# Residual rows by a DRAM copy, a bias row by accumulating DMAs, and a margin behind the products in TensorE's order

## The chip, the cores and the metric

The kernel runs on one core of one Trainium2 chip. The time is the device time of one execution in microseconds (us). Profiles are of one execution each; their times count from the start of the profiled span.

## The reference

One layer in which attention and a dense branch run side by side on the same normalised input (S = 2048 tokens, D = 640, bf16):

```python
xn = layernorm(x)                        # over D
# A: 32 heads of width 20; each position looks at 8 positions, 2 apart, backwards
q, k, v = split(xn @ wqkv)
logits[h,s,w] = (q[h,s] . k[h,s-2w]) * 20**-0.5      # s-2w < 0 is masked
o[h,s] = sum_w softmax_w(logits)[h,s,w] * v[h,s-2w]
# B: dense, F = 1536
h = gelu(xn @ w1 + b1)
out = x + o @ wo + h @ w2 + b2
```

The change concerns the terms `x + ... + b2` and the place of the logits in TensorE's queue.

## The kernel before

The 2048 tokens are cut into four chunks (`NCH`, number n) of 512, and each chunk into four blocks (`BPC`, number bl) of 128 tokens. The last of the 16 blocks has the number `LASTB` = 15. Everything between the first loads and the last store is held as small pieces of work, each with a name, an engine, an estimated duration, a rank, the pieces it needs and the buffers it holds. `make_plan` lists them; `Plan.run` plays them through with these numbers, at each moment giving a free engine the ready piece of lowest rank, and so fixes the order of TensorE, VectorE and ScalarE. That order is issued as it is (`manual_schedule` with these three engines). When a piece really takes longer than its estimate, the queues don't rearrange: the engine stands at the piece whose turn it is. SP (plain DMAs) and GpSimd, called POOL in profiles, are not in that set. Of a piece's needs on another engine the plan adds a small lag (0.22, 0.08 and 0.1 us behind TensorE, VectorE and ScalarE).

The pieces of a chunk, with their names:

- `st`, `rs`, `rc`, `xn`: mean and variance, square root, reciprocal, normalised rows (VectorE, ScalarE). `tp`, `tc`: transposes on TensorE and their copy to SBUF (`xnT`).
- `pj`, `pc` (chunk 0: `gj`, `gc`): the projections q, k, v (L428 and L445 in the profile) and their eviction. `pad`: the 14 columns ahead of a chunk's k and v, copied from the chunk before, or set to zero by a memset on POOL (L468) for chunk 0.
- `qk`: for each of the 8 offsets a product of q with the shifted k on VectorE (L478, tile `prod`). `lg`: four pieces per chunk, each sums two such products per head on TensorE into the logits `L` (L490).
- `m`, `mx`, `ex`, `ss`, `ri`, `at`: the softmax (maximum on VectorE L513, exponential on ScalarE, sum on TensorE L538, reciprocal and product on VectorE).
- `xd`: four DMAs from SP that spread the weights over the partitions of the heads' columns (L559, tile `ax`; there is one buffer of it).
- `av`, `ad`, `ot`: weights times shifted v (L569), additions (L578), and the attention output `oT` (L584), on VectorE.
- `f1`, `ge`: the dense branch's first product (L591) and GELU (L602). `o`: five pieces per block that accumulate h @ w2 and o @ wo in PSUM (L623, L624). `oc`, `od`: eviction to `osb` and the store.

The terms x and b2 come in at two places. Piece `xb` (one per chunk, L403) adds the broadcast row b2 to the chunk's x in SBUF, and for blocks below `LASTB` SP then stores the result to the output (L412, 15 stores in all). `od` later adds each block's `osb` to these rows by an accumulating DMA from POOL (L636). For the last block, x + b2 goes into PSUM by a product with the identity instead, and `osb` is stored plainly. So each piece `o` of a chunk needs `xb` of that chunk.

The loads stand at the start, ahead of the identity matrix and the constants that POOL makes (L317 to L325 and the helper make_identity). SP issues, in this order: x of chunk 0 and wqkv, b1, the rest of x, w1, the row b2 to all partitions (`b2bc`), w2, wo.

Of the kernel before, what the change touches and what calls it, by code (L numbers as in the profile page):

```python
# [11 lines left out]
ALU = mybir.AluOpType  # L12
# [3 lines left out]
PE, VE, SE, DQ = "pe", "ve", "se", "dq"  # L16


class Plan:
# [13 lines left out]
    def pool(self, name, n):  # L33
        self.pools[name] = n

    def add(self, name, engine, us, rank, needs, fn, bufs=(), after=0.0, table=None):
        t = {
            "name": name,
            "eng": engine,
            "us": us,  # L40
            "rank": rank,
            "needs": list(needs),
            "fn": fn,
            "bufs": list(bufs),
            "after": after,
            "table": table,
            "i": len(self.tasks),
        }
        self.tasks.append(t)
        self.by[name] = t  # L50
        for b in bufs:
            self.bufs.setdefault(b, set()).add(name)
        return name

    def run(self):
        end, left, held = {}, list(self.tasks), {p: {} for p in self.pools}
        remaining = {b: set(u) for b, u in self.bufs.items()}
        free = {PE: 0.0, VE: 0.0, SE: 0.0, DQ: 0.0}
        now, started, table = 0.0, [], "sqrt"
        running = []  # L60
        while left:
            done = [t for t in running if t["end"] <= now + 1e-9]
            for t in done:
                running.remove(t)
                for b in t["bufs"]:
                    remaining[b].discard(t["name"])
                    if not remaining[b]:
                        held[b[0]].pop(b, None)
            moved = True
            while moved:  # L70
                moved = False
                for eng in (PE, VE, SE, DQ):
                    if free[eng] > now + 1e-9:
                        continue
                    best = None
                    for t in left:
                        if t["eng"] != eng or t["after"] > now:
                            continue
                        if best is not None and (t["rank"], t["i"]) >= (best["rank"], best["i"]):
                            continue  # L80
                        if any(
                            n not in end
                            or end[n] + (self.LAG[self.by[n]["eng"]] if self.by[n]["eng"] != eng else 0.0) > now + 1e-9
                            for n in t["needs"]
                        ):
                            continue
                        new = {}
                        for b in t["bufs"]:
                            if b not in held[b[0]]:
                                new[b[0]] = new.get(b[0], 0) + 1  # L90
                        if any(len(held[p]) + k > self.pools[p] for p, k in new.items()):
                            continue
                        best = t
                    if best is not None:
                        left.remove(best)
                        best["start"], best["end"] = now, now + best["us"]
                        if best["table"] not in (None, table):
                            table = best["table"]
                            best["end"] += self.TABLE
                        end[best["name"]] = best["end"]  # L100
                        free[eng] = best["end"]
                        for b in best["bufs"]:
                            held[b[0]][b] = True
                        running.append(best)
                        started.append(best)
                        moved = True
            nxt = [f for f in free.values() if f > now + 1e-9]
            nxt += [
                e + self.LAG[self.by[n]["eng"]]
                for n, e in end.items()  # L110
                if e + self.LAG[self.by[n]["eng"]] > now + 1e-9
            ]
            nxt += [t["after"] for t in left if t["after"] > now + 1e-9]
            if left and not nxt:
                raise RuntimeError("no piece can start: " + ", ".join(t["name"] for t in left[:8]))
            if left:
                now = min(nxt)
        return started


S, D, F, H, W, DIL = 2048, 640, 1536, 32, 8, 2
P = 128
DH = D // H
PAD = (W - 1) * DIL
KT, FT = D // P, F // P
CH = 512
NCH = S // CH
BPC = CH // P
# [5 lines left out]
LASTB = S // P - 1  # L134
# [5 lines left out]
def make_plan(fns):  # L140

    pl = Plan()
# [6 lines left out]
    def f(kind, *a):  # L149
        return lambda: fns[kind](*a)  # L150
# [6 lines left out]
    for n in range(NCH):  # L157
        base = n * PERIOD
# [4 lines left out]

        for bl in range(BPC):
            land = (3.2, 3.2, 6.6, 6.6)[bl] if n == 0 else 11.4 + 1.9 * n
            pl.add(f"st{n}{bl}", VE, 1.1, -40 if n else -99, [], f("st", n, bl), after=land)
            if n == 0:
                pl.add(f"rs{n}{bl}", SE, 0.35, -99, [f"st{n}{bl}"], f("sqrt", n, bl, bl + 1), table="sqrt")
                pl.add(f"rc{n}{bl}", VE, 0.17, -99, [f"rs{n}{bl}"], f("rstd", n, bl, bl + 1))
# [3 lines left out]
        for bl in range(BPC):  # L173
            xn, tp = ("xn", n, bl), ("acc", "tp", n, bl)
            pl.add(f"xn{n}{bl}", VE, 0.42, early - 4 if n else -99, [f"rc{n}{bl}" if n == 0 else f"rc{n}"], f("xn", n, bl), [xn])
            pl.add(f"tp{n}{bl}", PE, 0.3, early - 3 if n else -99, [f"xn{n}{bl}"], f("tp", n, bl), [xn, tp])
            pl.add(f"tc{n}{bl}", SE, 0.65, early - 3 if n else -99, [f"tp{n}{bl}"], f("tc", n, bl), [tp, xnT])
        pl.add(f"xb{n}", VE, 1.5, base + 30, [f"xn{n}{bl}" for bl in range(BPC)], f("xb", n), after=31.0)

        if n == 0:  # L180
            for bl in range(BPC):
                for g, parts in enumerate(GROUPS):
                    ps, last = ("acc", "g", bl, g), max(p[0] for p in parts)
                    tos = sum(p[2] - p[1] for p in parts)
                    land = (5.9, 9.2, 11.5)[last]
                    r = -50 + (last == 2)
                    pl.add(f"gj{bl}{g}", PE, 0.28 * tos, r, [f"tc0{bl}"], f("gj", bl, g), [xnT, ps], land)
                    pl.add(f"gc{bl}{g}", SE, (0.27, 0.54, 0, 0.54)[tos - 1], -50, [f"gj{bl}{g}"], f("gc", bl, g), [ps] + [(q, k, v)[p[0]] for p in parts])
        for which, buf in enumerate((q, k, v)):
            for to in range(KT if n else 0):  # L190
                ps = ("acc", "p", n, which, to)
                r = early + (0 if which < 2 else 20)
                pl.add(f"pj{n}{which}{to}", PE, 1.08, r, [f"tc{n}{bl}" for bl in range(BPC)], f("pj", n, which, to), [xnT, ps])
                pl.add(f"pc{n}{which}{to}", SE, 0.52, early, [f"pj{n}{which}{to}"], f("pc", n, which, to), [ps, buf])
            if which:
                need = done(n - 1, which) if n else []
                bufs = [buf] + ([("k" if which == 1 else "v", n - 1)] if n else [])
                pl.add(f"pad{n}{which}", SE, 0.26, early if n else -50, need, f("pad", n, which), bufs)

        L = ("L", n)  # L200
        for wp in range(W // 2):
            pr = ("prod", "qk", n, wp)
            for i in range(2):
                need = done(n, 0) + done(n, 1) + [f"pad{n}1"]
                pl.add(f"qk{n}{wp}{i}", VE, 1.47, base + 3 * wp + i, need, f("qk", n, wp, i), [q, k, pr])
            pl.add(f"lg{n}{wp}", PE, 0.6, n - 1000, [f"qk{n}{wp}{i}" for i in range(2)] + ([f"lg{n}{wp-1}"] if wp else []), f("lg", n, wp), [pr, L])

        e, at, ax = ("e", n), ("attn", n), ("ax", n)
        m, rs, ss = ("m", n), ("rs", n), ("acc", "ss", n)
# [9 lines left out]
        for wp in range(W // 2):  # L219
            for i in range(2):  # L220
                need = [f"xd{n}", f"pad{n}2"] + done(n, 2)
# [11 lines left out]
        for bl in range(BPC):  # L233
            ob = ("osb", n, bl)
            O = [("O", n, bl)] if n < NCH - 1 or bl % 2 == 0 else [("acc", "lo", n, bl), ("acc", "hi", n, bl)]
            last = None
            for pc in range(5):
                need = [last] if last else [f"ge{n}{ft}" for ft in range(FT)] + [f"xb{n}"]
                if pc == 4:
                    need.append(f"ot{n}")  # L240
                us = (0.82, 0.82, 0.82, 1.1 if (n, bl) == (NCH - 1, BPC - 1) else 0.82, 1.37)[pc]
                last = pl.add(f"o{n}{bl}{pc}", PE, us, base + PERIOD + 8 + 8 * bl, need, f("o", n, bl, pc), O + (hTs if pc == 0 else hTs[3 * pc : 3 * pc + 3] if pc < 4 else [oT]), 31.0)
            pl.add(f"oc{n}{bl}", SE, 0.78, base, [last], f("oc", n, bl), O + [ob])
            pl.add(f"od{n}{bl}", SE, 0.0, base, [f"oc{n}{bl}"], f("od", n, bl), [ob])
# [4 lines left out]
def kernel(  # L249
# [16 lines left out]
    nc = tc.nc  # L266
    assert tuple(A_x.shape) == (1, S, D) and tuple(B_w1.shape) == (D, F)

    x_sd = A_x.rearrange("b s d -> (b s) d")
# [36 lines left out]
        cs = slice(n * BPC, (n + 1) * BPC)  # L306
        nc.sync.dma_start(x_sb[:, cs, :], x_nb[:, cs, :])
    nc.sync.dma_start(w1_sb[:], B_w1.rearrange("(t p) n -> p t n", p=P))
    nc.sync.dma_start(b2bc[:], b2_bcast)
    nc.sync.dma_start(w2_sb[:], B_w2.rearrange("(t p) n -> p t n", p=P))  # L310
    nc.sync.dma_start(wo2[:], A_wo.rearrange("(p t) n -> p t n", t=KT))


    ident = consts.tile([P, P], BF16, name="ident")
# [83 lines left out]
            tiles["tp", n, bl][:, 0 : KT * P].rearrange("p (t m) -> p t m", t=KT),  # L398
        )

    def do_xb(n):
        cs = slice(n * BPC, (n + 1) * BPC)
        nc.vector.tensor_tensor(  # L403
            out=x_sb[:, cs, :],
            in0=x_sb[:, cs, :],
            in1=b2bc[:].unsqueeze(1).to_broadcast([P, BPC, D]),
            op=ALU.add,
        )
        for bl in range(BPC):
            b = n * BPC + bl  # L410
            if b < LASTB:
                nc.sync.dma_start(out_sd[b * P : (b + 1) * P, :], x_sb[:, b, :])  # L412


    def qkv_tile(n, which):
# [259 lines left out]
```

## Time and profile before

| | us |
|---|---|
| median of three runs | 235.9 |
| lowest and highest of them | 233.46 and 236.65 |
| the profiled execution | 233.1 |
| its span | 231.1 |

| engine | busy us | share of the span |
|---|---|---|
| TensorE, products | 213.3 | 92% |
| VectorE | 171.7 | 74% |
| ScalarE | 109.2 | 47% |
| GpSimd | 14.5 | 6% |

PE is TensorE, PEld its weight load, DVE VectorE, ACT ScalarE; "SPq" is SP's queue. A line such as "PE L L490 <- DVE prod L478: 4.6, 3, 2.6" in the list of waits says that TensorE stood for 4.6 us in three places before instructions of line 490 until VectorE had finished those of line 478, at most 2.6 us at once. In the chain of waits (the work that ended last, followed back from the end) each line has a start, a duration and what took the time. In the timeline the number in brackets is the time for which the engine was idle just before, and who ended that. Of the rows of slices, each digit is a fortieth of the span (5.8 us) in tenths of busy time.

### The profile page before, as it was taken

The numbers are of one execution on the slowest core, as the hardware profiler recorded it, in microseconds if no ns is written. First come the engines' busy times: TensorE is split into PE (matmuls) and PEld (weight loads), VectorE is DVE, ScalarE is ACT, GpSimd is POOL, SyncE is SP. The second block draws the span as 40 slices with busy tenths as digits, with TensorE's granted clock in tenths as the row PEclk, the third lists the DMA queues.
The fourth block names the chain that finished last, engine by engine and source line by source line (L and its number), as shares of the span: only waits on it lengthen the run. The fifth ranks groups of instructions, "written<-read, shape, count | busy, mean of one in ns | idle before, by whom it ended". The sixth has DMA issues, their size and how long they took to land.

```text
span 231.1 us, 4042 instructions
## 1 busy us (share of the span) xinstructions
PE 213.3 (92%) x1728; PEld 124.3 (54%) x1754; DVE 171.7 (74%) x170; ACT 109.2 (47%) x193; POOL 14.5 (6%) x33
## 2 busy tenths in 40 slices
PE   0999999999999869999899999997999999899993
PEld 0899744665555434465455555453555554455551
DVE  4767999680899999987899959999975129994000
ACT  3476794885755617624285652620078331161211
POOL 2000000000000001010000010100011101011220
PEclk9999999999999999999999999999999999999999
DMA  6999900339200002018020540202041742022232
GB/s 231 369 370 387 365 18 0 118 118 204 89 0 0 0 0 31 0 16 187 12 28 0 102 111 0 28 3 28 0 116 11 137 96 30 0 28 31 28 32 53
DMA packets 13417, 19.52 MB, mean 84 GB/s; under 512 B 984, under 2 KB 10584, under 8 KB 13400
## 3 DMA queue, kind: packets, MB, share of 16 engines
q1 hardware_dynamic: 11096, 16.65, 23.6%
q0 software_dynamic: 2160, 2.46, 8.7%
q8 instruction: 13, 0.21, 0.4%
q10 hardware_dynamic: 144, 0.16, 0.2%
q14 instruction: 4, 0.03, 0.0%
HBM read 10.00 MB, written 5.08 MB: 65 GB/s over the span
## 4 chain that ended last, share of the span: by engine, by line
PE 55%; DVE 26%; issue 7%; DMA 5%; ACT 4%; SPq 2%; ACTq 0%; DVEq 0%
PE lo L623 16%; PE hps L591 12%; DVE pv L569 10%; PE gps L445 8%; DVE pv L578 7%; PE pps L428 7%; PE hi L624 5%; DMA ax<-attn 4%; DVE prod L478 3%; PE L L490 3%; SPq L559 2%; DVE oT L584 1%; PE tp L392 1%; DMA x_sb<-in_A_x_dram 1%; ACT L602 1%
## 5 line engine op out<-in xcount | busy, mean ns | idle before, releaser
L569 DVE TENSOR_TENSOR pv<-vT,ax 128x2560 bf16<-128x2560 bf16 x32 | 45.7, 1485 | 20.4 <-DMA ax<-attn 20.4
L591 PE MATMUL hps<-xnT,w_sb 128*128 128x512 bf16 x232 | 54.4, 380 | 0.9 <-ACT hT L602 0.4
L623 PE MATMUL lo<-w_sb,hT 128*128 128x512 bf16 x183 | 52.8, 379 | 0.7 <-ACT osb L629 0.7
L478 DVE TENSOR_TENSOR prod<-qT,kT 128x2560 bf16<-128x2560 bf16 x32 | 45.4, 1481 | 0.0
L624 PE MATMUL hi<-w_sb,hT 128*128 128x128 bf16 x192 | 42.1, 219 | 0.6 <-issue 0.2
L629 ACT CAST osb<-lo 128x512 bf16<-128x512 f32 x16 | 9.4, 585 | 62.0 <-issue 35.3
L602 ACT ACTIVATE hT<-hps,b1T 128x512 bf16<-128x512 f32 x48 | 31.6, 688 | 14.0 <-PE hps L591 13.2
L591 PEld LDWEIGHTS <-w_sb 128*128 128x128 bf16 x240 | 22.4, 98 | 26.8 <-issue 2.1
L578 DVE TENSOR_TENSOR pv<-pv 128x5120 bf16<-128x5120 bf16 x12 | 33.9, 2824 | 0.4
L623 PEld LDWEIGHTS <-hT 128*128 128x128 bf16 x192 | 18.7, 98 | 22.5 <-issue 0.6
L636 POOL DMA_DIRECT2D out_dram<-osb x15 | 13.1, 873 | 209.5 <-ACT osb L630 209.5
L623 PE MATMUL lo<-wo,oT 128*128 128x512 bf16 x76 | 22.7, 379 | 0.0
L624 PEld LDWEIGHTS <-hT 128*128 128x128 bf16 x192 | 18.8, 98 | 2.2 <-issue 0.8
L624 PE MATMUL hi<-wo,oT 128*128 128x128 bf16 x80 | 17.5, 219 | 0.2
L428 PE MATMUL pps<-xnT,wv_sb 128*128 128x512 bf16 x73 | 16.8, 380 | 0.1
L428 PE MATMUL pps<-xnT,wk_sb 128*128 128x512 bf16 x74 | 16.6, 379 | 0.1
L428 PE MATMUL pps<-xnT,wq_sb 128*128 128x512 bf16 x73 | 16.6, 379 | 0.1
L490 PE MATMUL L<-prod,head_of 128*32 128x256 bf16 x320 | 11.5, 274 | 4.6 <-DVE prod L478 4.6
L396 ACT COPY xnT<-tp 128x640 bf16<-128x640 bf16 x16 | 10.4, 701 | 7.3 <-PE tp L392 7.3
L463 ACT CAST vT<-pps 128x512 bf16<-128x512 f32 x15 | 8.8, 588 | 9.7 <-PE pps L428 9.7
L623 PEld LDWEIGHTS <-oT 128*128 128x128 bf16 x80 | 7.8, 98 | 9.5
L428 PEld LDWEIGHTS <-wk_sb 128*128 128x128 bf16 x75 | 8.8, 117 | 7.4
(64 smaller groups left out, 200.1 us busy)
## 6 DMA issues: line engine op xcount, KB each, us to landing
ax<-attn SPq DMA_DIRECT2D x16, 256.0 KB, 4.7
w_sb<-in_B_w_dram SPq DMA_DIRECT2D x2, 1920.0 KB, 15.5
out_dram<-x_sb SPq DMA_DIRECT2D x15, 160.0 KB, 2.2
out_dram<-osb POOLq DMA_DIRECT2D x15, 160.0 KB, 3.3
x_sb<-in_A_x_dram SPq DMA_DIRECT2D x3, 640.0 KB, 10.2
wq_sb<-in_A_wqkv_dram SPq DMA_DIRECT2D x1, 800.0 KB, 4.7
wk_sb<-in_A_wqkv_dram SPq DMA_DIRECT2D x1, 800.0 KB, 7.1
wv_sb<-in_A_wqkv_dram SPq DMA_DIRECT2D x1, 800.0 KB, 8.8
```

The source lines that it names most:

```text
L396: nc.scalar.copy(xnT[:, :, bl * P : (bl + 1) * P], tiles["tp", n, bl][:, 0 : KT * P].rearrange("p (t m) -> p t m", t=KT),)
L428: nc.tensor.matmul(ps[:], lhsT=wqkv_p[which][:, ti, to, :], rhs=xnT[:, ti, :], start=(ti == 0), stop=(ti == KT - 1),)
L445: nc.tensor.matmul(ps[:, i, :], lhsT=wqkv_p[which][:, ti, to, :], rhs=tiles["xnT", 0][:, ti, cs], start=(ti == 0), stop=(ti == KT - 1),)
L478: nc.vector.tensor_tensor(out=prod[:, i, :, :], in0=qkv_tile(n, 0)[:], in1=qkv_tile(n, 1)[:, :, off : off + CH], op=ALU.mult,)
L490: nc.tensor.matmul(L[j * H : (j + 1) * H, 2 * wp : 2 * wp + 2, :], lhsT=head_of[:], rhs=prod[:, :, t, j * P : (j + 1) * P], start=(t == 0 ...
L569: nc.vector.tensor_tensor(out=pv[:, i, :, :].rearrange("p t (j c) -> p t j c", j=BPC), in0=qkv_tile(n, 2)[:, :, off : off + CH].rearrange( ...
L578: nc.vector.tensor_tensor(out=ta[:], in0=ta[:], in1=tb[:], op=ALU.add)
L591: nc.tensor.matmul(ps[:], lhsT=w1_sb[:, ti, ft * P : (ft + 1) * P], rhs=tiles["xnT", n][:, ti, :], start=(ti == 0), stop=(ti == KT - 1),)
L602: nc.scalar.activation(hT[:], tiles["hps", n, ft][:], ACT.Gelu_apprx_tanh, bias=b1T[:, ft : ft + 1], scale=1.0)
L623: nc.tensor.matmul(lo[:], lhsT=lhs, rhs=rhs[:, 0:CH], start=first, stop=last)
L624: nc.tensor.matmul(hi[:, 0 : D - CH], lhsT=lhs, rhs=rhs[:, CH:D], start=first, stop=last)
L636: nc.gpsimd.dma_start(rows, tiles["osb", n, bl][:], accum_op=ALU.add)
```

## The change

Three parts.

1. The output rows below the last block are filled by four DMAs from DRAM to DRAM on SP (512, 512, 512 and 384 rows of x), placed behind the loads. Four accumulating DMAs on POOL then add b2 to them, with the row in DRAM, repeated, as their source; each writes the rows of one copy and so comes after it. In the text both stand ahead of the constants. The load of `b2bc` moves behind wo.
2. `xb` is left for the last block alone (128 rows), and the stores in it go. Only the last block's pieces `o` need it.
3. A piece can have a `slack`: the plan holds it back until that long after the end of what it needs. `lg` gets 0.8. The plan's estimate of `st` goes from 1.1 to 1.17, and that of `xb` from 1.5 to 0.5.

```diff
-    def add(self, name, engine, us, rank, needs, fn, bufs=(), after=0.0, table=None):
+    def add(self, name, engine, us, rank, needs, fn, bufs=(), after=0.0, table=None, slack=0.0):
...
+            "slack": slack,
...
                         if any(
                             n not in end
-                            or end[n] + (self.LAG[self.by[n]["eng"]] if self.by[n]["eng"] != eng else 0.0) > now + 1e-9
+                            or end[n] + t["slack"] + (self.LAG[self.by[n]["eng"]] if self.by[n]["eng"] != eng else 0.0) > now + 1e-9
                             for n in t["needs"]
                         ):
...
-            pl.add(f"st{n}{bl}", VE, 1.1, -40 if n else -99, [], f("st", n, bl), after=land)
+            pl.add(f"st{n}{bl}", VE, 1.17, -40 if n else -99, [], f("st", n, bl), after=land)
...
-        pl.add(f"xb{n}", VE, 1.5, base + 30, [f"xn{n}{bl}" for bl in range(BPC)], f("xb", n), after=31.0)
+        if n == NCH - 1:
+            pl.add("xb", VE, 0.5, base + 30, [f"xn{n}{BPC - 1}"], f("xb"), after=31.0)
...
-            pl.add(f"lg{n}{wp}", PE, 0.6, n - 1000, [...], f("lg", n, wp), [pr, L])
+            pl.add(f"lg{n}{wp}", PE, 0.6, n - 1000, [...], f("lg", n, wp), [pr, L], slack=0.8)
...
-                need = [last] if last else [f"ge{n}{ft}" for ft in range(FT)] + [f"xb{n}"]
+                need = [last] if last else [f"ge{n}{ft}" for ft in range(FT)] + (["xb"] if (n, bl) == (NCH - 1, BPC - 1) else [])
...
-    nc.sync.dma_start(b2bc[:], b2_bcast)
     nc.sync.dma_start(w2_sb[:], B_w2.rearrange("(t p) n -> p t n", p=P))
     nc.sync.dma_start(wo2[:], A_wo.rearrange("(p t) n -> p t n", t=KT))
+    nc.sync.dma_start(b2bc[:], b2_bcast)
+
+    for r in range(0, LASTB, BPC):
+        rows = slice(r * P, min(r + BPC, LASTB) * P)
+        nc.sync.dma_start(out_sd[rows, :], x_sd[rows, :])
+    for r in range(0, LASTB, BPC):
+        n_rows = min(BPC, LASTB - r) * P
+        nc.gpsimd.dma_start(
+            out_sd[r * P : r * P + n_rows, :],
+            bass.AP(tensor=B_b2.tensor, offset=B_b2.offset, ap=[[0, n_rows], [1, D]]),
+            accum_op=ALU.add,
+        )
...
-    def do_xb(n):
-        cs = slice(n * BPC, (n + 1) * BPC)
-        nc.vector.tensor_tensor(
-            out=x_sb[:, cs, :],
-            in0=x_sb[:, cs, :],
-            in1=b2bc[:].unsqueeze(1).to_broadcast([P, BPC, D]),
-            op=ALU.add,
-        )
-        for bl in range(BPC):
-            b = n * BPC + bl
-            if b < LASTB:
-                nc.sync.dma_start(out_sd[b * P : (b + 1) * P, :], x_sb[:, b, :])
+    def do_xb():
+        nc.vector.tensor_tensor(out=x_sb[:, LASTB, :], in0=x_sb[:, LASTB, :], in1=b2bc[:], op=ALU.add)
```

In `Plan.run`, the moments at which the plan looks again are extended by each value of slack that occurs.

More of the change, by code (lines that the diff above doesn't have):

```diff
@@ L59, in run @@
         now, started, table = 0.0, [], "sqrt"
-        running = []
+        running, slacks = [], {t["slack"] for t in self.tasks}
         while left:
@@ L107, in run @@
             nxt = [f for f in free.values() if f > now + 1e-9]
[L108 to L112, printed above, removed]
+            for late in slacks:
+                ready = [e + late + self.LAG[self.by[n]["eng"]] for n, e in end.items()]
+                nxt += [r for r in ready if r > now + 1e-9]
             nxt += [t["after"] for t in left if t["after"] > now + 1e-9]
@@ L205, in make_plan @@
                 pl.add(f"qk{n}{wp}{i}", VE, 1.47, base + 3 * wp + i, need, f("qk", n, wp, i), [q, k, pr])
-            pl.add(f"lg{n}{wp}", PE, 0.6, n - 1000, [f"qk{n}{wp}{i}" for i in range(2)] + ([f"lg{n}{wp-1}"] if wp else []), f("lg", n, wp), [pr, L])
+            pl.add(f"lg{n}{wp}", PE, 0.6, n - 1000, [f"qk{n}{wp}{i}" for i in range(2)] + ([f"lg{n}{wp-1}"] if wp else []), f("lg", n, wp), [pr, L], slack=0.8)
         e, at, ax = ("e", n), ("attn", n), ("ax", n)
```

## The prediction

> **What bounds the kernel now.** I read the page first (busy shares, slices), then the waits, then the chain, and last the timelines of DVE, PE and POOL and short windows of the DMA.
>
> ```profile
> PE 213.3 (92%) x1728; PEld 124.3 (54%) x1754; DVE 171.7 (74%) x170; ACT 109.2 (47%) x193; POOL 14.5 (6%) x33
> DMA  6999900339200002018020540202041742022232
> q0 software_dynamic: 2160, 2.46, 8.7%
> ```
>
> PE is busy for 213.3 of 231.1 us. Of the 17.8 us that are left, 6.0 lie ahead of the first transpose and 3.8 behind the last product; some 8 us in the middle are all that any reordering of TensorE can give back. The DMA engines are full until about 29 us and lightly used after that. Queue 0 (the accumulating stores) took 8.7% of 16 engines for 2.46 MB.
>
> ```profile
> DVE pv L569 <- DMA ax<-attn: 20.4, 4, 9.3
> PE L L490 <- DVE prod L478: 4.6, 3, 2.6
> ```
>
> Two waits matter. DVE waits for the expanded attention weights (ax) once per chunk. PE waits for products ahead of the logits, 4.6 us in three places. The chain ties the first of each together:
>
> ```profile
> 51.81 1.24 SPq L559
> 53.09 5.44 DMA ax<-attn
> 58.61 5.71 DVE pv L569 x4
> 64.35 2.82 DVE pv L578
> 67.17 5.62 DVE pv L569 x4
> 72.81 2.83 DVE pv L578
> 75.67 2.84 DVE pv L578
> 78.53 1.49 DVE oT L584
> 80.03 2.81 DVE prod L478 x2
> 82.88 0.73 PE L L490 x20
> ```
>
> From 51 to 83 us there is only SP, DMA and DVE on it: when the first ax lands later, the next chunk's first logits are later by as much, and PE, which has run out of earlier work at 80.25, stands. This is the stretch to watch. Next, what the bias additions cost today, from the timeline of DVE:
>
> ```profile
> 38.45 0.80 DVE L378 TENSOR_SCALAR xn<-x_sb,mv,rstd 128x640 bf16<-128x640 bf16 x2
> 39.17 0.17 DVE L370 RECIPROCAL rstd<-std 128x4 f32<-128x4 f32 x1
> 39.26 1.46 DVE L403 TENSOR_TENSOR x_sb<-x_sb,b2bc 128x2560 bf16<-128x2560 bf16 x1
> 42.23 1.23 DVE L513 TENSOR_REDUCE m<-L 128x128 bf16<-128x1024 f32 x1 [1.52 <-PE L L500]
> ```
>
> The first addition is followed by 1.52 us of idle DVE; the second (45.14) by a wait of 0.82 for the sum; the third (50.82) by 6.30 for ax; the fourth (168.90) ends at 170.4, as the logits that its successor needs end. All four are in slack.
>
> [...] the ax transfer with an accumulating store inside it (SP issue at 179.8) kept DVE waiting until 189.05, 9.3 us, against 8.2 us for the first. [...] no copy from DRAM to DRAM is in this trace. [...]
>
> **The change, part by part.**
>
> *Bias additions.* Four DVE operations of 1.47 us become one on a fifth of the row, about 0.4. Gain 0, as their slack shows; if one had no cover, 1.47 each.
>
> *SP.* Fifteen stores of x go (332 to 1448 ns of SP each, at 40.7, 54.8 and 170.4). Four copies come behind wo, and b2bc moves behind wo. SP is done with wo at 21.3 us and next needed for ax at 50.45: 29 us for five issues. Even at 2 us each, as b2bc took (2.06), that is 10 us; cost 0. b2bc landed at 23.35, w1 at 22.9: broadcasting one DRAM row costs the engines no more than a load, and b2bc is wanted only for the last block. w2, wanted at 44.5, comes 0.5 us earlier.
>
> *POOL.* Four accumulating DMAs come first in the text, each waiting for a copy. Behind them in the text stand the identity, the constants and the two memsets of the k and v padding. In this profile POOL does not follow the text:
>
> ```profile
> 0.74 0.20 POOL masks.py:197 MEMSET ident<- 128x128 bf16 x1 [0.29 <-POOLq L659]
> 0.88 0.10 POOL L317 MEMSET eps_t<- 128x1 f32 x1
> 0.91 0.11 POOL L321 MEMSET ones_r<- 1x32 bf16 x1
> 0.97 0.20 POOL L323 MEMSET maskrow<- 1x128 bf16 x1
> 1.21 0.28 POOL masks.py:199 TENSOR_SCALAR_AFFINE_SELECT ident<-ident 128x128 bf16<-128x128 bf16 x1
> ```
>
> The select, which must wait for its memset, stands behind three memsets that the text has after it. Work that is ready is put first, so I expect all memsets ahead of the accumulations. Next on POOL are the stores of osb at 88.0, long after. Cost 0; if the order is otherwise, see the third case.
>
> *DMA.* The first weights end at 28.8 us (share 0.26 in the last half microsecond):
>
> ```profile
> 28.50:29.00 0.50, 0.50 (x4) 0.24 (x3) 0.50 (x2) 0.49 (x2) 0.00 (x0) 1.00 0.26 102
> ...
> 178.50:179.00 0.50, 0.50 (x6) 0.27 (x5) 0.46 (x1) 0.32 (x1) 0.00 (x0) 1.00 1.11 97
> 179.00:179.50 0.50, 0.50 (x5) 0.29 (x4) 0.50 (x1) 0.00 (x0) 0.00 (x0) 1.00 0.97 141
> 179.50:180.00 0.50, 0.50 (x5) 0.31 (x4) 0.27 (x1) 0.00 (x0) 0.00 (x0) 1.00 0.57 90
> ...
> 51.50:58.50 7.00, 7.00 (x34) 3.84 (x33) 0.81 (x1) 3.87 (x7) 0.00 (x0) 1.00 0.87 204
> ```
>
> The last two columns are the share of the 16 engines and GB/s. Copies: 15 x 163,840 B = 2.46 MB. At the 340 GB/s of the stores of x (42.0 to 43.5) they take 7.2 us, [...] Accumulations: one osb store of 128 rows fills the engines for (1.11 + 0.97 + 0.57) x 0.5 = 1.33 us; the bias adds to 1,920 rows, 15 times that, 20 us. Their source is DRAM, which the trace does not show: half of this if the source was the dear side, half as much again if it is dearer; I take 20. While the first accumulation waits, later copies use the engines, so there is no hole: 28.8 + 9.5 + 20 = 58.3 us. The first ax begins to move at 51.5 and wants 7.0 x 0.87 = 6.1 us of the engines. 6.8 us of accumulation are then left; sharing evenly, ax lands about 6 us late. Bounds: 0 (accumulation at half price ends at 48) and 9 (half as dear again[...]).
>
> *Margin on the logits, and statistics counted 1.17 instead of 1.1 in the plan.* No work is added; PE's order changes. Twelve statistics move the plan's first products 0.84 us later, and the logits stand at least 0.8 behind their products. Of the three PE waits (2.63 at 82.88, 1.68 at 160.62, 0.34 at 163.42) the first gets one projection (five products, 1.08 us) and perhaps a piece of w2 (0.82) ahead of it: 1.1 to 1.9, I take 1.5. Worked by hand, the plan has the fourth chunk's first logits 1.1 us behind their products already and its second 0.4: I take 0.3 there. Gain 1.8. In return the first chunk's last logits, which the softmax waits for (1.52 above), go one piece later (1.08); short waits behind them on PE (the sum at 47.49 starts 0.5 after the exponential) take up a part, so 0.7 lost, bounds 0 and 1.1.
>
> *Sum.* +6.0 (first ax) + 0.7 - 1.8 = +4.9 us. What is late next: DVE from 58.6 to 91 has no hole in which to recover, and PE from 83 to 158 hardly any. The profiled execution took 233.1 us (span 231.1 and 2.0 around it) and becomes 238.0, 2.1% more. The median of the runs is 235.9, 2.8 above the profiled one; with the same offset I predict 240.8.
>
> **Rivals.**
>
> *First, the forecast* (0.52): the accumulations overlap the first ax. Its own range, with 3 to 9 us for the delay: 237.8 to 243.8.
>
> *Second, they are over in time* (0.25). For it: the slices from 29 to 40 us are empty, and price and start are both mine. Against: it needs copies and accumulations in 22.7 us, where I count 29.5. Then 0.7 - 1.8: 234.8 us, not slower.
>
> *Third, POOL is held up* (0.15): the memsets of the padding end up behind the accumulations, which wait for the copies. For it: the text's order. Against: the lines above. The last copy lands at about 40 us, four issues (at least 0.86 each) follow or are under way, and the first products, at 27.08 today, start near 42. That is 15 us; the clash with ax is then gone, as ax comes after it. 235.9 + 15 - 1.8 = 249. If the identity too is behind them, 35 us or more (0.02).
>
> *Fourth, faster* (0.06): no clash, and the new order of TensorE removes most of its 8 us of idle time in the middle: 230.5. Against: three waits make up 4.6 of it, and 0.8 is less than each of the two large ones.
>
> **How the numbers follow.** A measurement of this kernel tells about 2% from no change, 4.7 us. Slower: 0.6 of the forecast, the third case, the identity: 0.48. Same: the rest of the forecast and nearly all of the second: 0.44. Faster: the fourth and a little of the second: 0.08. The range goes from just under the second case to the third: 234.0 to 249.5.
>
> **What would show it.** In the profile after: queue 0 with twice the rows and near 17% of the engines; DMA slices full from 29 to about 60 us; the first pv at about 65 instead of 58.6; the wait of PE for prod at the second chunk of 5 to 7 us. If pv starts before 60, the second case holds; if the first prod starts after 35, the third. That DVE loses 5.5 us of work should move nothing. I am wrong altogether if the end moves while the first pv stays.

## The result, and the profile after

The changed kernel takes 245.38 us (median of four runs, 245.21 to 245.45), the kernel before 234.68 in the same measurement (233.25 to 236.65): 4.5% slower, ratio 1.0449 with a 95% interval of 1.0355 to 1.0543. Forecast were 240.8 us and 234.0 to 249.5: the direction and the place were right, the size was about half (4.9 us forecast, 10.7 measured by the medians).

First the page of the changed kernel: busy times, then PE's slices, its granted clock, the DMA's slices, and the row of the accumulating queue.

```profile
span 243.4 us, 4026 instructions
PE 217.2 (89%) x1727; PEld 124.5 (51%) x1754; DVE 166.8 (69%) x167; ACT 108.5 (45%) x193; POOL 18.6 (8%) x37
PE   0899999999999332999999999999999999989993
PEclk9999999999999955699999999999999999999998
DMA  7999979889960000100452018020220281122222
q0 software_dynamic: 4144, 4.92, 20.9%
```

The span of the profiled execution grew by 12.3 us. Of these, 8.4 are idle time of PE (243.4 - 217.2 = 26.2 against 17.8 before) and 3.9 are longer busy time for the same products. Both sit in slices 13 to 17, counted from 0 (79 to 110 us): a hole in PE's row and, a little behind it, a clock of 0.5. DVE lost 4.9 us of work, and nothing came of it. The DMA's slices, which before were empty from 29 to 40 us and lightly used later, are now nearly full to 72.

The waits of the changed kernel (total, times, longest in us):

```profile
DVE pv L570 <- DMA ax<-attn: 33.2, 4, 20.0
ACT vT L471 <- DVE pv L570: 8.8, 1, 8.8
PE L L491 <- DVE prod L479: 6.9, 1, 6.9
PE pps L429 <- ACT vT L464: 5.9, 1, 5.9
```

One wait of DVE for ax is now 20.0 us; the same wait of the first chunk was 6.3 before, and the longest of any chunk 9.3. The other three lines are what it leads to, as the chain shows from the end of the first softmax (start, duration, what):

```profile
50.29 1.23 DVE attn L549
...
56.41 15.31 DMA ax<-attn
71.84 5.71 DVE pv L570 x4
77.57 2.82 DVE pv L579
...
91.75 1.49 DVE oT L585
93.25 2.81 DVE prod L479 x2
96.10 1.26 PE L L491 x15
```

The last of the four transfers of the first ax takes 15.31 us instead of 5.44. The first pv (the first product of weights and shifted v, piece `av`) starts at 71.84 instead of 58.61: 13.2 us later, of which 1.1 are the later softmax (attn starts at 50.29, before at 49.20) and 12.1 the transfer. From there every line to the second chunk's logits is as long as before and stands 13 us later. In the windows of the DMA (the last three columns are PE's clock, the share of the 16 engines, and GB/s):

```profile
36.00:44.00 8.00, 7.95 (x96) 3.99 (x96) 4.05 (x8) 3.90 (x7) 1.96 (x2) 1.00 0.89 73
44.00:52.00 8.00, 7.89 (x70) 5.29 (x71) 5.39 (x10) 7.18 (x11) 0.00 (x0) 1.00 0.79 70
52.00:60.00 8.00, 8.00 (x39) 4.33 (x38) 0.00 (x0) 4.35 (x8) 0.00 (x0) 1.00 1.02 71
60.00:72.00 12.00, 11.89 (x59) 6.61 (x59) 0.16 (x1) 7.19 (x13) 0.00 (x0) 1.00 0.95 150
```

The accumulations move 70 to 73 GB/s, and when the first ax is issued, at 51.54, nothing is added to that for 8 us. By the trace's packet records no packet of SP's queue ends between 36.5 and 61.2 us; those of the accumulating queue run from 35.4 to 71.8. In the kernel before, with nothing in its way, the first packet of ax ends 1.4 us after the issue. So here ax doesn't get a share of the engines: it gets nothing for 8 us, and after that moves its 1.05 MB in 10.2 us beside the rest of the accumulations.

### The profile page after: what moved, and what is told of

Its sections match the earlier page's. It is cut to its first block, busy times and chain, and to the rows that moved or that the text cites. A ratio compares the mean times of both kernels' runs of the same rounds, so it can differ in the third digit from the quotient of the medians.

```text
span 243.4 us, 4026 instructions
## 1 busy us (share of the span) xinstructions
PE 217.2 (89%) x1727; PEld 124.5 (51%) x1754; DVE 166.8 (69%) x167; ACT 108.5 (45%) x193; POOL 18.6 (8%) x37
## 4 chain that ended last, share of the span: by engine, by line
PE 58%; DVE 17%; DMA 9%; issue 6%; ACT 5%; SPq 3%; ACTq 0%; DVEq 0%
PE lo L624 18%; PE hps L592 17%; DMA ax<-attn 8%; PE gps L446 7%; DVE pv L570 7%; PE hi L625 6%; PE pps L429 5%; DVE pv L579 5%; PE L L491 3%; SPq L560 3%; ACT xnT L407 2%; DMA x_sb<-in_A_x_dram 1%; DVE prod L479 1%; ACT L603 1%; DVE attn L549 1%
## 5 line engine op out<-in xcount | busy, mean ns | idle before, releaser
L592 PE MATMUL hps<-xnT,w_sb 128*128 128x512 bf16 x233 | 55.7, 385 | 0.8 <-ACT hT L603 0.4
L429 PE MATMUL pps<-xnT,wv_sb 128*128 128x512 bf16 x74 | 17.8, 395 | 5.9 <-ACT vT L464 5.9
L625 PE MATMUL hi<-wo,oT 128*128 128x128 bf16 x80 | 18.0, 225 | 0.6 <-issue 0.2
L491 PE MATMUL L<-prod,head_of 128*32 128x256 bf16 x320 | 12.2, 283 | 6.9 <-DVE prod L479 6.9
L429 PEld LDWEIGHTS <-wv_sb 128*128 128x128 bf16 x75 | 8.8, 118 | 13.7 <-issue 6.9
L491 PEld LDWEIGHTS <-head_of 128*32 128x32 bf16 x320 | 7.4, 98 | 13.7 <-issue 13.4
L407 ACT COPY xnT<-tp 128x640 bf16<-128x640 bf16 x16 | 10.2, 704 | 6.0 <-PE tp L403 6.0
## 6 DMA issues: line engine op xcount, KB each, us to landing
x_sb<-in_A_x_dram SPq DMA_DIRECT2D x3, 640.0 KB, 10.2
```

What stands on the lines that cost most here:

```text
L407: nc.scalar.copy(xnT[:, :, bl * P : (bl + 1) * P], tiles["tp", n, bl][:, 0 : KT * P].rearrange("p (t m) -> p t m", t=KT),)
L429: nc.tensor.matmul(ps[:], lhsT=wqkv_p[which][:, ti, to, :], rhs=xnT[:, ti, :], start=(ti == 0), stop=(ti == KT - 1),)
L491: nc.tensor.matmul(L[j * H : (j + 1) * H, 2 * wp : 2 * wp + 2, :], lhsT=head_of[:], rhs=prod[:, :, t, j * P : (j + 1) * P], start=(t == 0 ...
L592: nc.tensor.matmul(ps[:], lhsT=w1_sb[:, ti, ft * P : (ft + 1) * P], rhs=tiles["xnT", n][:, ti, :], start=(ti == 0), stop=(ti == KT - 1),)
L625: nc.tensor.matmul(hi[:, 0 : D - CH], lhsT=lhs, rhs=rhs[:, CH:D], start=first, stop=last)
```

## The experiments

Theory A: the accumulations keep the first ax transfer from the DMA engines. Rival B: the new order of TensorE and the missing additions cost the time. Later the question became what makes the accumulations so slow, and whether they cost anything where no ax transfer is under way.

### Take the accumulations away

```diff
-    for r in range(0, LASTB, BPC):
-        n_rows = min(BPC, LASTB - r) * P
-        nc.gpsimd.dma_start(out_sd[...], <row b2, repeated>, accum_op=ALU.add)
```

> The changed kernel without its four accumulating DMAs of b2 (b2 is left out of all rows but the last block's). Theory A, the accumulations keep the first ax transfer from the DMA engines: the first pv comes back from 71.8 to 59-60 us, TensorE keeps its full clock, and the time is 233 to 235. Theory B, the new order of TensorE and the missing additions cost the time: pv and time stay within 2 us of the changed kernel (243 to 247).

Measured: 231.41 us, ratio to the kernel before 0.984 (0.978 to 0.990); first pv at 59.31; clock 1.0.

```profile
59.31 5.70 DVE L563 TENSOR_TENSOR pv<-vT,ax 128x2560 bf16<-128x2560 bf16 x4 [7.09 <-DMA ax<-attn]
```

Without the accumulations the 10.7 us are gone, and 2 to 4 more (2.1 by the profiled spans, 231.1 and 229.0; 4.4 by the medians): the rest of the change is a gain, larger than A's 233 to 235 had it.

### Only the new order, and only the margin

```diff
-            pl.add(f"lg{n}{wp}", PE, 0.6, ..., [pr, L])
+            pl.add(f"lg{n}{wp}", PE, 0.6, ..., [pr, L], slack=0.8)
...
-            pl.add(f"st{n}{bl}", VE, 1.1, ...)
+            pl.add(f"st{n}{bl}", VE, 1.17, ...)
```

> The kernel before with only the margin of 0.8 behind the products and the statistics counted 1.17; x and b2 are handled as before. A: 233.5 to 236, the same as before, first pv at 59-60 (the softmax about 1 us later). B: 240 or more.

> The kernel before with only the margin of 0.8 (statistics counted 1.1 as before). If the margin alone gives the gain of the order: 230.9 to 232 and TensorE's wait for prod near 1.3 us in all. If the later statistics matter too: between that and 235.8; if it needs both: 234 or more.

Measured: 231.23 us with both (0.984, 0.977 to 0.990; first pv at 61.11, later than the 59 to 60 expected), 231.90 with the margin alone (0.987, 0.981 to 0.994). So the margin gives most of it, and the removed additions nothing that shows: this kernel still has them. In the timeline of PE the large stall before the second chunk's logits, 2.63 us before, becomes with the margin alone

```profile
84.81 0.73 PE L489 MATMUL L<-prod,head_of 128*32 128x256 bf16 x20 [0.61 <-DVE prod L477]
```

and a new one of 2.06 us appears before the product with the maximum (115.09). B has fallen; the 233.5 to 236 expected with both was also too high.

### Only the DMA part

```diff
-        pl.add(f"xb{n}", VE, 1.5, ...)      # all four stay in the plan as before;
+    def do_xb(n):                            # their function is empty but for the last
+        if n < NCH - 1:
+            return
```

> The changed kernel with the order of TensorE, VectorE and ScalarE as before (no margin, 1.1, and empty pieces where the removed additions stood); the copies and accumulations as in the change. A: first pv at 70 to 72 (the softmax is 1 us earlier), time 244 to 246.5, since without the margin TensorE stands a little longer. B: 234 to 237.

Measured: 249.39 us, ratio 1.059 (1.052 to 1.066), first pv at 71.27. The clash is that of the change, but the kernel is slower than it, by 4.0 us by the medians and 2.3 by the profiled spans (245.7 and 243.4). The waits differ so:

```profile
PE L L492 <- DVE prod L480: 17.6, 3, 15.4
```

With the old order PE stands 15.4 us in one piece, where the changed kernel stands 5.9 and 6.9 with five products in between. I had expected 244 to 246.5: the order was worth more than my 1.8 us here, where it acts on a larger stall.

### What the accumulations read

```diff
# e4: source in SBUF
-            bass.AP(tensor=B_b2.tensor, offset=B_b2.offset, ap=[[0, n_rows], [1, D]]),
+            b2bc[:].unsqueeze(1).to_broadcast([P, nb, D]),
# e5: the terms exchanged
+        nc.sync.dma_start(out_sd[...], <row b2, repeated>)
+        nc.gpsimd.dma_start(out_sd[rows, :], x_sd[rows, :], accum_op=ALU.add, max_dma_last_dim=1280)
# e9: 16 rows of DRAM, each read 32 times
+            bass.AP(tensor=A_x.tensor, offset=A_x.offset, ap=[[D, 16], [0, n_rows // 16], [1, D]]),
```

> The changed kernel with the accumulations' source in SBUF (the broadcast tile b2bc) instead of the row in DRAM; four DMAs of the same rows. If the DRAM source makes them dear (A1): they run at the 120 GB/s of the osb stores, 20 us, end at 56 to 57 instead of 62, first pv at 65 to 67, time 239 to 241. If the price lies in reading and writing the output rows (A2): 26 us as in the change, pv at 71 to 72, time 245.

Measured: 230.81 us (0.983, 0.975 to 0.990), first pv at 58.87. The accumulations from SBUF ran at 197 GB/s, faster than either reading of the source had it:

```profile
38.00:48.00 10.00, 9.89 (x109) 5.75 (x109) 4.41 (x12) 7.04 (x10) 0.69 (x1) 1.00 1.18 197
```

They end at 50.0 us, and ax comes after them. (The expectation has the accumulations of the change end at 62 us after 26; by the packet records above they end at 71.8 after 36.) Their number, their bytes and what they do to the output rows are those of the change, which moved 70 to 73 GB/s; so here accumulation into DRAM as such is not what is slow.

> The changed kernel with the two terms exchanged: the repeated row b2 is copied plainly to the output rows by SP, and the rows of x, each a different place in DRAM, are added by the accumulating DMAs (512, 512, 512, 384 rows of 1280 B). If reading one row again and again is what made the accumulations slow (R): they run at 150 to 200 GB/s, are over by 52, first pv at 59 to 60, time 231 to 233. If a DRAM source as such is slow for an accumulation (D): 70 to 80 GB/s again, pv at 70 to 72, time 244 to 246. The plain copy of the repeated row should take more time than the copy of x under R, about as much under D.

Measured: 243.99 us (1.039, 1.032 to 1.046), first pv at 72.02. The time is as under D, the traffic as under R: it is now the plain copy of the repeated row, on SP's queue and with no accumulation, that crawls,

```profile
30.00:38.00 8.00, 7.54 (x66) 3.51 (x68) 8.00 (x6) 7.46 (x11) 0.00 (x0) 1.00 0.88 77
38.00:46.00 8.00, 7.91 (x93) 3.92 (x82) 4.05 (x9) 4.29 (x7) 1.22 (x1) 1.00 0.74 79
```

and by the packet records lasts until 63.2 us, about 34 us, where the copy of x took 7.9. The expectation under R forgot that the slow part would only change places. The late pv has two parts here. The first ax is issued at 58.69 instead of 51.54, since the softmax is late. And it stands behind the copy in the same queue: DVE waits 13.0 us for it, 7.1 without accumulations. What delays the softmax is PE, which stood still from 46 to 50 us, for which the profile names no releaser ("issue" 4.1 us), and then had a clock of 0.57 to 54. The queue that carries instructions moved its third packet of 16 KB at 47.7 us, where the other traces have it at 30 to 35. So PE may have waited for instructions that the copy held up; that was not tried.

> The changed kernel with the accumulations' source changed from the one row b2 to 16 neighbouring rows of x, each read 32 times (24 in the last DMA), same destination and number of rows; what is added is x's first 16 rows instead of b2. If the slowness comes from all engines reading one place (H): 150 to 200 GB/s, first pv near 59 to 61, time 230 to 233. If it comes from reading any row again and again (Q): 70 to 80 GB/s, pv at 70 to 72, time 244 to 246.

Measured: 230.45 us (0.983, 0.975 to 0.992; two runs), first pv at 59.53. With 16 rows instead of one, everything else alike:

```profile
38.00:40.00 2.00, 2.00 (x10) 0.78 (x8) 1.96 (x6) 0.69 (x1) 0.07 (x1) 1.00 1.18 193
40.00:42.00 2.00, 2.00 (x27) 1.04 (x27) 0.04 (x1) 0.69 (x1) 0.00 (x0) 1.00 1.18 198
```

198 GB/s, against 70 to 73 in the change. So DRAM as a source is not slow here, nor is reading a row 32 times; slow is one row as the source of everything. Nor is this row slow from the start: in the swapped kernel the first 200 packets from it, with the 128 that fill b2bc, took 55 ns each, and after them the median of a hundred lies between 99 and 241 ns until 57 us. Every slow kernel read b2, though. That one row of x, repeated, is as slow was not tried, nor which part of the memory sets the limit.

### The same accumulations elsewhere

```diff
     def do_xd(n):
...
+        if n == 0:
+            <the four copies and the four accumulations>
...
-    engines = {PE, DVE, Activation}
+    engines = {PE, DVE, Activation, SP}          # and POOL too in the second of these kernels
```

> The changed kernel with copies and accumulations issued behind the four DMAs of the first ax (SP's queue is held in that order); the same source, rows and price. If only the clash with the first ax costs time: first pv at 59 to 60, the accumulations are over at 85 to 90, the first osb store waits for its own rows alone, time 231 to 233 like the kernel without accumulations. If the accumulations cost time wherever they are (HBM or POOL held up): above 238.

Measured: 246.61 us (1.049, 1.041 to 1.056), as slow as the change. The first pv is at 60.10, as expected, but POOL's timeline shows that its queue did not keep my order:

```profile
62.99 1.22 POOL L560 DMA_DIRECT2D out_dram<-in_B_b_dram  x1 [61.02 <-DMA out_dram<-in_A_x_dram]
87.60 0.91 POOL L638 DMA_DIRECT2D out_dram<-osb  x1 [23.39 <-ACT osb L632]
88.16 1.41 POOL L560 DMA_DIRECT2D out_dram<-in_B_b_dram  x1
101.41 0.89 POOL L638 DMA_DIRECT2D out_dram<-osb  x1 [11.84 <-ACT osb L632]
101.95 2.38 POOL L560 DMA_DIRECT2D out_dram<-in_B_b_dram  x2
```

Accumulations were placed between osb stores and waited behind these. The last two started at 101.95, just ahead of the second ax (issued from 104.85), and the clash of the change came again one chunk later:

```profile
125.91 1.49 DVE L571 TENSOR_TENSOR pv<-vT,ax 128x2560 bf16<-128x2560 bf16 x1 [17.16 <-DMA ax<-attn]
```

An accident, but one that moves the loss with the clash. With POOL's order held as well, all four are issued between 63 and 70 us:

> As the kernel with copies and accumulations behind the first ax, but with POOL's order held too, so that all four accumulations come before the first osb store: same source, rows and price, now at about 62 to 88 us, between the first and the second ax. If the loss is the clash with an ax transfer alone: pv of both chunks undisturbed (60 and 112), time 231 to 233. If the dear accumulations cost time by themselves: 238 or more.

Measured: 231.36 us (0.987, 0.981 to 0.993). First pv at 60.26, the second chunk's at 112.49:

```profile
112.49 1.49 DVE L571 TENSOR_TENSOR pv<-vT,ax 128x2560 bf16<-128x2560 bf16 x1 [3.59 <-DMA ax<-attn]
```

The accumulations are as slow as ever, 63 to 79 GB/s,

```profile
70.00:74.00 4.00, 4.00 (x20) 2.19 (x19) 4.00 (x4) 2.29 (x4) 0.00 (x0) 1.00 1.02 70
78.00:82.00 4.00, 4.00 (x20) 2.21 (x19) 3.97 (x3) 2.38 (x5) 0.00 (x0) 1.00 1.08 68
```

take 35 us from the first packet to the last landing (66.1 to 101.7, with an osb store of 1.3 us of the engines among them), and cost nothing that shows, since no transfer that an engine waits for is issued then: the time is that of the kernel without accumulations (231.41). The clash is the whole loss.

### Smaller accumulations

```diff
-    for r in range(0, LASTB, BPC): ... n_rows = 512, 512, 512, 384
+    for b in range(LASTB): ... 128 rows each
```

> The changed kernel with its four accumulations cut into fifteen of 128 rows (same row of DRAM as the source, same bytes). No packet of the first ax moved before about 60 us, when three of the four were through. If an engine serves queue 0 one whole DMA at a time before it turns (W): ax gets its turn after at most 8 rows an engine, pv at 62 to 66, time 237 to 241. If all that is queued goes first, or the rows' slowness blocks every queue (B): pv at 70 to 73, time 244 to 247.

Measured: 245.32 us (1.047, 1.038 to 1.056; two runs), first pv at 72.13. Cutting them changes nothing in the time: the first packet of ax ends at 59.6 us, 8.1 after its issue (9.6 in the change). W has fallen. Why ax gets nothing for 8 us, rather than a share, is open.

### The halved clock by itself

```diff
     def do_lg(n, wp):
...
+        if n == 1 and wp == 0:
+            for _ in range(14):
+                nc.tensor.matmul(L[:, 0:4, :], lhsT=ident[:], rhs=w2_sb[:, 0, 0:CH], start=True, ...)
```

> The changed kernel with 14 more products (128x512, into the logits' bank, overwritten by the first real one) ahead of the second chunk's first logits, where TensorE stands for 6.9 us. If the halved clock behind the stall costs about 2.5 us of its own: the clock is back near 96 us instead of 102, and the time is 242.5 to 243.5. If the clock follows something else, or the work at half clock was hidden: 245 to 246, the fillers lie in the stall and cost nothing.

Measured: 243.91 us (1.041, 1.031 to 1.051), a median 1.5 us below the changed kernel's 245.38; the profiled spans are 241.5 and 243.4. Three of the four executions took 243.6 to 244.0, the fourth 246.4. With the 14 more products the clock is back at 92 to 94 us, with nothing but fillers and waiting behind it,

```profile
90.00:92.00 2.00, 2.00 (x6) 0.73 (x5) 1.97 (x2) 0.00 (x0) 0.00 (x0) 0.50 0.00 0
92.00:94.00 2.00, 1.56 (x7) 0.58 (x6) 2.00 (x2) 0.00 (x0) 0.00 (x0) 0.98 0.00 0
```

while the changed kernel ran at half clock until about 102:

```profile
100.00:102.00 2.00, 2.00 (x7) 0.54 (x4) 2.00 (x3) 1.91 (x3) 0.88 (x1) 0.50 0.03 8
```

So with these 14 products in the queue the clock came back some 10 us sooner: that is shown. That it also saves time is likely, 1.5 to 1.9 us and so under the 2.5 that I had set, but it isn't settled: the intervals of the two kernels overlap, and one execution with the fillers is slower than any of the changed kernel.

### A version that beats both

The kernel with the accumulations' source in SBUF already beats both. One more number of the plan was wrong by the profile of before: an ax transfer counts 5.0 us there and takes 8.2.

```diff
-        pl.add(f"xd{n}", DQ, 5.0, ...)
+        pl.add(f"xd{n}", DQ, 8.2, ...)
```

> The kernel with the accumulations' source in SBUF, and the plan's duration of an ax transfer raised from 5.0 to the 8.2 us seen in the profile of before. If the plan's optimism still leaves TensorE standing (1.0 us before logits and 0.8 before the maximum's product): 229 to 230.5. If the order is no longer what bounds it: 230.5 to 231.5, no difference.

Measured: 229.63 us, ratio to the kernel before 0.980 (0.973 to 0.987); the waits of PE for prod are gone from the list. Against the same kernel with 5.0 the intervals overlap (0.983, 0.975 to 0.990), so that what the last step adds, 1.2 us by the medians, is likely but not settled.

## Why the prediction was right in direction and half in size

- **Place and mechanism: right.** Accumulations that aren't over when the first ax is issued, DVE late by that, PE standing before the second chunk's logits. Taking them away, speeding them up or moving them each brings the time to 230.5 to 231.5. That 245.4 lay inside the range is in part luck: the forecast's own range ended at 243.8, and the upper end, 249.5, came from the third case, which didn't happen.
- **Bias additions and the queues of SP and POOL: right.** No gain from the four additions; SP was done with its copies at 25.1 us; the memsets of the padding stood at 1.73 us, ahead of the accumulations. The third case (POOL held up) has fallen.
- **"I take 20" us for the accumulations: the step that failed.** They take about 34 us when no ax is in their way (the 35 above less one osb store). The upper bound, half as much again, was too low as well. It was the step before it that misled: from b2bc landing 0.45 us behind w1 I read that "broadcasting one DRAM row costs the engines no more than a load". That holds for those 128 reads, 55 ns a packet; the change reads the row 1,920 times, and it was after some 200 that the swapped kernel's reads became slow. The bound should have been left open upwards for a pattern of access that the trace did not show at that length. Below, the guess erred too: from SBUF the same accumulations take 14.4 us (35.6 to 50.0).
- **9.5 us for the copies: too long, and without effect.** It was an estimate of mine that the trace of before did not show. By the packet records they ran from 28.6 to 36.5 us: 7.9 us, or 313 GB/s, close to the 7.2 reckoned from the stores of x. The accumulations began at 35.4.
- **"Sharing evenly": wrong.** For the first 8 us ax got nothing. The even share was an assumption of mine that no trace of before had shown. Together with the duration this made 12.1 us of delay for the transfer, forecast 6.0, bound 9; pv started at 71.84, forecast about 65.
- **The stall of PE: 12.8 us in two pieces, forecast 7.8 (2.63 + 6.0 + 0.7 less 1.5).** The first piece has a route that I hadn't followed: the copy of v's padding on ACT waits until pv has read the old v (8.77 us), evictions queue behind it, and PE finds no free PSUM (5.86).
- **Not foreseen: the clock.** 0.5 from 85.1 to 102.2 us, and 3.9 us of busy time more.
- **Gain of the order: forecast 1.1 net (1.8 less 0.7), measured 2.1 by the profiled spans (231.1 and 229.0) and 4 by the medians.** The loss was as said: the softmax 1.1 us later. Why the gain was undersized is not shown; that a stall of 2.6 us costs more than its length in some executions would fit (below).

## What to carry to other kernels

In this kernel, work handed to the DMA engines was free only where nothing that an engine waits for was issued before it ended (231.36 us with the accumulations between two ax transfers and 231.41 without any, against 245.38 with the first ax issued into them); add up its time from its start to the next such transfer, and let the estimate be open upwards for any pattern of access that the trace doesn't show at that size. The constant that 1,920 rows need was better read from DRAM once and then taken from SBUF (230.81 us against 245.38). In this fixed order of issue, a margin behind a slower engine's result cost little where other work filled it (231.90 us with the margin alone, against 235.28); that it pays twice where stalls bring the clock down was not shown.

## What the hardware showed beyond that

- One 1280-byte row of DRAM as the source of 1,920 rows gave 70 to 73 GB/s in the change and 63 to 79 behind the first ax, where the DMA accumulates, and 77 to 79 in the swapped kernel from 30 to 50 us, where it copies (windows of 4 to 8 us); 16 neighbouring rows gave 190 to 200, and SBUF 197. The first 200 reads of the row in the swapped kernel took 55 ns each; the packets of 1280 bytes that the kernel before loads in its first 30 us have a median of 58.
- In these kernels such reads held up other queues. From the issue of an ax transfer to the end of its first packet it took 9.6 us in the change, 8.1 with fifteen accumulations and 8.4 at the second chunk of the kernel whose accumulations slipped behind osb stores, against 1.4 in the kernel before. In the swapped kernel it went the other way round: the first accumulation, issued at 39.90, moved its first packet at 54.9, behind SP's copy. After that both queues move.
- TensorE's granted clock fell to 0.5 some 4 us after it ran out of work (in the change idle from 81.0, half clock from 85.1; 3.7 to 4.9 us in five such stalls) and came back 2.7 to 6.1 us after work began again (in the change 96.1 and 102.2, in the kernel with only the DMA part 95.5 and 98.7). By the trace's clock records these stretches at half clock lasted 3.41 us in the swapped kernel, 6.83 with the fillers, 13.65 with only the DMA part and 17.07 in the change.
- The kernel before may sit at the edge of this. Its executions beside the last group of experiments took 233.27, 233.53 and 233.73 us at a clock of 1.0, and 234.38 to 235.88 at 0.993. By estimate one stretch at half clock as long as the 3.41 us of the swapped kernel gives just that (1.7 us in 231 is 0.7%). Kernels with the margin and no clash ran at 0.996 to 1.0, but for two of the four executions with the margin alone (0.993). That the stall of 2.63 us, grown a little, is what lowers it in some executions fits, but wasn't tried by itself.
